# A gated linear recurrence and a squared-ReLU network on one core: a chunk's columns in another order, and the orders of VectorE and TensorE written by hand

## The chip, the core and the metric

The kernel runs on one core of a Trainium2 chip. Times are device microseconds (us) of one execution; the time of a kernel is the median of its runs. The engines are TensorE (PE; its weight loads are listed as PEld), VectorE (DVE), ScalarE (ACT), GpSimd (POOL) and SyncE (SP), which here issues transfers. Each works through its own list of instructions in order.

## What is computed

The reference, cut to what matters (batch 4, 8 heads, 768 steps, head size 48; the network takes 384 to 2048 to 384 over 3072 tokens):

```python
scale = np.minimum(mag, 0.999) / (mag + 1e-06)          # mag = |a_re + i a_im|
a_re_n, a_im_n = a_re * scale, a_im * scale
for t in range(S):
    new_re = ar * S_re - ai * S_im                      # ar, ai: step t of a_re_n, a_im_n
    new_im = ar * S_im + ai * S_re
    S_re, S_im = new_re + einsum('bhd,bhe->bhde', k[:, :, t], v[:, :, t]), new_im
    y[:, :, t] = einsum('bhd,bhde->bhe', q[:, :, t], S_re)
x = y with the heads side by side                       # 3072 x 384
h = np.maximum(x @ w_in, 0.0)
out = (h * h) @ w_out
```

## The kernel before

**Tiling.** A sequence of 768 steps is cut into 6 chunks of 128 steps (`C`). The 8 heads of a chunk lie as 4 pairs, a pair on 128 partitions with 48 rows and a gap of 16 for each head; the gaps of three pairs hold the rows of the fourth, so `NG` = 3 column blocks carry 4 pairs. Two chunks of different sequences make a group (`GC` = 2), so there are 12 groups (`NGR`), 256 tokens each; groups 0 to 5 run through one pair of sequences, 6 to 11 through the other. Within a chunk, 8 neighbouring steps make a block (`L` = 8, `NB` = 16 blocks).

**Operands of a group** (`make_operands`). ACT and DVE turn the gates of a group into running products along time. `steps_in_blocks` multiplies along a block, 7 steps in all, each a product `pr` of 384 elements and two writes of 96; the columns it takes, step `j` of every block, lie 8 elements apart in `raw`. A scan of 12 pieces makes the scale factors, four levels of doubling (`while m < NB`) join the 16 blocks of a chunk, ACT copies the carries, and a complex product over 1344 elements (`inner`) applies them. The last products write `qk`, the decayed queries and keys (four rows of 128 columns per block); six DMAs on SP's queue move the rows of the fourth pair into `last`.

**Attention of a chunk** (`chunk`, a generator with two stops). PE multiplies the state of the chunk before (`y<-qk,state_mm` and `y<-last,state_mm`), then queries and keys into the scores `a_ps`; DVE masks them into `a`; PE adds `a` times the values `vt` to `y`, and ACT copies `y` to `x`. Then PE transposes the keys (`tp`), ACT copies them to `kt`, PE makes `add`, and DVE joins it to the `state` (the last chunk of a sequence leaves this out).

**The network.** `first_product` makes `h_ps`, 8 pieces of 6 matrix products of 256 columns (each two passes in the trace), from `x`, whose gaps six DMAs fill (`fill_gaps`, `x<-x`); ACT applies ReLU and square. `second_product` makes `o_ps`, 16 products of 384 columns for each of the two chunks; ACT copies the result to `o`, and SP stores it. The weights come as 64-bit numbers; DVE decodes them in 16 pieces (`weights`, five instructions each), the first 8 for `h_ps`, the others for `o_ps`.

**What sets the order.** Through groups 0 and 1 DVE's list is the order of the code (`manual_schedule`); everything else, and DVE from group 2 on, is ordered by a scheduler. `attention(gi)`, `first_product(gi - 1)` and `second_product(gi - 1)` are written one after the other for each group.

**PSUM banks.** `a_ps` 2, `y` 1, `tp` and `add` together 2, `h_ps` 2, `o_ps` 1.

Of the kernel before, what the change touches and what calls it, by code (L numbers as in the profile page):

```python
# [11 lines left out]

# [402 lines left out]
def quotient_path(ctx, tc, feat, vtok, w_in, w_out, w1, w2, out, n_seq, good):  # L415
# [23 lines left out]
    tmp = ctx.enter_context(tc.tile_pool(name="tmp", bufs=1))  # L439
    att = ctx.enter_context(tc.tile_pool(name="att", bufs=2))  # L440
# [10 lines left out]
    def pads(hh):  # L451
        return gap_rows(hh, D)
# [10 lines left out]
    vt = [const.tile([C, HH * NP, ROWS], F32, name=f"vt{i}") for i in range(2 * GC)]  # L463
    for t in vt:
        nc.gpsimd.memset(t, 0.0)

    def load_parts(gi, parts, gaps):

        for b, n in enumerate(groups[gi]):
            for hh in range(HH):  # L470
                nc.sync.dma_start(
                    out=raw[gi % 2][rows(hh), parts, b].rearrange("d x g t -> d x (g t)"),
                    in_=feat[n, hh, :, parts, 0:NG].rearrange("d x g t -> d x (g t)"))
                rest = feat[n, hh].rearrange("(g r) x p t -> g r x p t", g=NG)
                for g in range(NG):
                    gaps.dma_start(out=raw[gi % 2][pads(hh), parts, b, g],
                                   in_=rest[g, :, parts, NG])

    def load_values(gi):
        for b, n in enumerate(groups[gi]):  # L480
            nc.sync.dma_start(out=vt[gi % 2 * GC + b][:, :, 0:D],
                              in_=vtok[n * C:(n + 1) * C].rearrange("c (h d) -> c h d", d=D))

    def load(gi):
        load_parts(gi, slice(A_RE, V), nc.sync)
        load_values(gi)

    load_parts(0, slice(A_RE, Q), nc.scalar)
    load_parts(0, slice(Q, V), nc.sync)
# [10 lines left out]
    nc.gpsimd.memset(mask, 1.0)  # L500
    nc.gpsimd.affine_select(out=mask, in_=mask, pattern=[[1, C]], compare_op=ALU.is_ge, fill=0.0,
                            base=0, channel_multiplier=-1)
# [98 lines left out]
    def make_operands(gi):  # L601
        r = raw[gi % 2].rearrange("p x b g t -> p x (b g t)")
        a = r[:, A_RE:A_IM + 1]
        ab = a.rearrange("p c (n j) -> p c n j", j=L)
        n = SEG * NB

        def steps_in_blocks(js):

            for j in js:
                x, w = ab[:, :, :, j - 1], ab[:, :, :, j]  # L610
# [13 lines left out]
                                       op1=ALU.add)  # L624
        nc.scalar.activation(out=z, in_=u, func=AF.Abs_reciprocal_sqrt)
# [13 lines left out]
                                       op1=ALU.mult)  # L639
        steps_in_blocks((5,))  # L640
        for x, y in ((u, low), (v, high)):
            for s in range(SEG):
                at = slice(s * C, (s + 1) * C)
                nc.vector.tensor_tensor_scan(out=x[:, at], data0=x[:, at], data1=y[:, at],  # L644
                                             initial=1.0, op0=ALU.mult, op1=ALU.mult)
        for i, x in enumerate((u, v)):
# [16 lines left out]
        inner = ab[:, :, :, 0:L - 1]  # L663
        cmul(inner, inner, spread(carry.rearrange("p c s n -> p c (s n)"), [n, L - 1]), [n, L - 1],
             [nrm.tile([P, 2, E], F32, tag=tag, name=tag)[:, :, 0:n * (L - 1)].rearrange(
                 "p c (n j) -> p c n j", j=L - 1) for tag in ("sq", "both")])

        qk, pd = qk_of[gi % 2], prod[gi % 2]
        shrink = ends[:, 0, gi].rearrange("p (b g) -> p b g", g=NG)
        for c in (RE, IM):  # L670
            tt(qk[:, c, :, :, C], raw[gi % 2][:, A_RE + c, :, :, C - 1], shrink, ALU.mult)
        steps = qk.rearrange("p x b g t -> p x (b g) t")[:, :, :, 0:C]
        a3 = a.rearrange("p x (s t) -> p x s t", t=C)
# [16 lines left out]
    def chunk(gi, b):  # L690
# [23 lines left out]
        yield  # L714
        am = []
        for hh in range(HH):
            am.append(att.tile([C, NP, C], F32, name="a", bufs=3))
            tt(am[hh], ps[hh], mask.unsqueeze(1).to_broadcast([C, NP, C]), ALU.mult)
        for p_ in range(NP):
            for hh in range(HH):  # L720
                nc.tensor.matmul(y[hh * ROWS:(hh + 1) * ROWS, p_], lhsT=v[:, HH * p_ + hh],  # L721
# [8 lines left out]

        for c in (RE, IM):
# [4 lines left out]
            nc.scalar.copy(  # L736
                out=kt[c][:, NG].rearrange("t (hh x) -> t hh x", hh=HH)[:, :, 0:D].rearrange(
                    "t hh (g r) -> t hh g r", g=NG),
                in_=tp.rearrange("t g (hh x) -> t hh g x", hh=HH)[:, :, :, D:ROWS])
        add = pm.tile([P, 2, NP, D], F32, tag="m", name="add")  # L740
        for c in (RE, IM):
            for p_ in range(NP):
                for hh in range(HH):
                    rr = slice(hh * ROWS, (hh + 1) * ROWS)
                    nc.tensor.matmul(add[rr, c, p_], lhsT=kt[c][:, p_, rr],  # L745
                                     rhs=v[:, HH * p_ + hh, 0:D], start=True, stop=True)
# [10 lines left out]
        p_ = tmp.tile([P, 2, NP, D], F32, tag="tp", name="p_")  # L757
# [38 lines left out]
    def store(i, b, ps):  # L796
# [3 lines left out]
        nc.sync.dma_start(out=out[n * C:(n + 1) * C], in_=o)  # L800

    def attention(gi):
        make_operands(gi)
        for b in range(GC):
            for _ in chunk(gi, b):
                pass
        if gi + 2 < NGR:
            load(gi + 2)
        fill_gaps(gi)

    def attention_among(gi, others):

        make_operands(gi)
        first, second = [chunk(gi, b) for b in range(GC)]
        for step, n in ((first, 3), (first, 0), (second, 2), (second, 0), (first, 1), (second, 0)):
            next(step, None)
            for _ in range(n):
                next(others)
        load(gi + 2)
        fill_gaps(gi)  # L820
# [3 lines left out]
    banks = {}  # L824

    def first_weights():
        for j in every:
            weights(j)
            yield

    def second_weights():
        for b, pool, tag in ((0, po, "o"), (1, ph, "h")):
            banks[b] = pool.tile([P, DM], F32, tag=tag, name="o_ps")
        for j in every:
            weights(NBLK + j)
            for b in range(GC):
                second_product(0, b, banks[b], [j])
            yield

    with tc.manual_schedule(engines={mybir.EngineType.DVE}):  # L840
        others = first_weights()
        attention_among(0, others)
        first_product(0, every[:6])
        for j in every[6:]:
            next(others)
            first_product(0, [j])
        others = second_weights()
        attention_among(1, others)
        for j in every[6:]:
            next(others)  # L850
            first_product(1, every[4 * (j - 6):4 * (j - 6) + 4])
        for b in range(GC):
            store(0, b, banks[b])
    for gi in range(2, NGR + 1):
        if gi < NGR:
            attention(gi)
# [79 lines left out]
```

## Time and profile before

| | |
|---|---|
| median of 3 runs | 823.46 us (821.85 to 823.92) |
| profiled execution | 823.65 us, of which the span of its trace is 821.9 us |
| mean granted clock of PE | 0.968 |
| PE busy | 695.2 us (85% of the span) |
| DVE busy | 497.7 us (61%) |
| ACT busy | 287.0 us (35%) |
| chain that ended last | PE 59%, DVE 31%, DMA 3%, issue 3%, ACT 3% |

Busy shares are means over stages of different kinds: decoding and first operands at the start, a mixture in the middle, matrix products alone at the end. PE's passes overlap, so a busy PE is not PE at its peak; where the text needs the cost of a pass it takes the start of one run of passes to the start of the next. A line L459 is the helper `tt`, by which nearly all DVE products are issued, so the rows go by tiles.

### The profile page before, as it was taken

What the parts mean: (1) busy time and instruction counts of PE and PEld (TensorE: products, weight loads), DVE (VectorE), ACT (ScalarE), POOL (GpSimd) and SP (SyncE); (2) the same over time, 40 slices, a digit from 0 to 9 for tenths busy, and PEclk for the clock granted to TensorE, in tenths of its full rate; (3) what the DMA queues carried; (4) which work ended last, traced back from release to release, by engine and by line L of the source; (5) the groups of instructions that cost most, each with busy time, mean ns of one, the idle gap of its engine ahead of it and who ended that gap; (6) DMA issues with size and microseconds to landing.
All of it is one profiled execution on the core that took longest, in us unless ns stands there. A gap on an engine that the chain in (4) does not pass through costs nothing.

```text
span 821.9 us, 10849 instructions
## 1 busy us (share of the span) xinstructions
PE 695.2 (85%) x4154; PEld 531.9 (65%) x4154; DVE 497.7 (61%) x1020; ACT 287.0 (35%) x558; POOL 7.7 (1%) x22
## 2 busy tenths in 40 slices
PE   0074319979897998998999989989999999999997
PEld 0063208658666866866858758768778678677673
DVE  4979999799798899999949479179113021010000
ACT  3145336335231624532525334334314224013130
POOL 3000000000000000000000000000000000000000
PEclk9999959999698999999999999999999999999999
DMA  5959807504324513242602501501002000000000
GB/s 122 161 101 187 165 7 167 125 15 78 48 59 82 84 38 78 53 82 45 105 17 46 82 24 32 86 23 34 12 20 45 10 10 6 10 14 2 20 0 25
DMA packets 68670, 47.65 MB, mean 58 GB/s; under 512 B 31616, under 2 KB 63488, under 8 KB 68608
## 3 DMA queue, kind: packets, MB, share of 16 engines
q1 hardware_dynamic: 68032, 46.66, 30.5%
q8 instruction: 35, 0.57, 0.3%
q10 hardware_dynamic: 576, 0.20, 0.1%
q14 instruction: 27, 0.22, 0.1%
HBM read 36.18 MB, written 4.72 MB: 50 GB/s over the span
## 4 chain that ended last, share of the span: by engine, by line
PE 59%; DVE 31%; DMA 3%; issue 3%; ACT 3%; SPq 1%; ACTq 0%; DVEq 0%
PE h_ps L782 25%; PE o_ps L793 22%; DVE raw L459 6%; DVE pr L459 5%; DVE sq L644 4%; PE a_ps L712 4%; PE y L721 3%; PE add L745 2%; DMA raw<-in_feat_dram 2%; PE y L705 2%; DVE a L459 2%; DVE qk L459 2%; DVE sq L459 1%; DVE both L544 1%; DVE state L459 1%
## 5 line engine op out<-in xcount | busy, mean ns | idle before, releaser
L782 PE MATMUL h_ps<-x,w 128*128 128x256 f32 x1152 | 262.5, 386 | 40.6 <-DMA x<-x 21.7
L782 PEld LDWEIGHTS h_ps<-x,w 128*128 128x128 f32 x1152 | 219.6, 193 | 75.6 <-issue 24.1
L793 PE MATMUL o_ps<-w,h 128*128 128x384 f32 x768 | 255.7, 491 | 4.3 <-DVE w L459 3.2
L793 PEld LDWEIGHTS o_ps<-w,h 128*128 128x128 f32 x768 | 145.2, 191 | 101.5 <-DVE w L459 3.3
L459 DVE TENSOR_TENSOR a<-a_ps,mask 128x512 f32<-128x512 f32 x48 | 30.9, 682 | 132.5 <-PE a_ps L712 132.5
L459 DVE TENSOR_TENSOR pr<-raw 128x384 f32<-128x384 f32 x84 | 71.7, 854 | 60.0 <-DMA raw<-in_feat_dram 59.0
L785 ACT ACTIVATE h<-h_ps 128x512 f32<-128x512 f32 x96 | 57.1, 594 | 91.6 <-PE h_ps L782 91.2
L712 PE MATMUL a_ps<-qk 48*128 48x128 f32 x576 | 51.1, 301 | 43.5 <-DVE qk L459 43.5
L712 PEld LDWEIGHTS a_ps<-qk 48*128 48x128 f32 x576 | 43.5, 203 | 49.8 <-DVE qk L459 43.5
L721 PE MATMUL y<-a,vt 128*64 128x128 f32 x384 | 41.6, 318 | 26.8 <-DVE a L459 26.7
L786 ACT ACTIVATE h<-h 128x512 f32<-128x512 f32 x96 | 60.4, 630 | 2.6
L799 ACT COPY o<-o_ps 128x384 f32<-128x384 f32 x24 | 11.5, 479 | 142.5 <-PE o_ps L793 142.4
L721 PEld LDWEIGHTS y<-a,vt 128*64 128x64 f32 x384 | 29.3, 157 | 37.0 <-DVE a L459 28.8
L459 DVE TENSOR_TENSOR raw<-pr 128x96 f32<-128x96 f32 x168 | 44.4, 331 | 8.0 <-ACT sq L619 6.2
L644 DVE TENSOR_TENSOR_SCAN sq<-sq,both 128x128 f32<-128x128 f32 x144 | 46.9, 400 | 1.1 <-ACT both L635 0.9
L901 DVE CAST count<-number 1x1 int32<-1x1 f32 x1 | 0.1, 145 | 72.5 <-PE number L900 72.5
L459 DVE TENSOR_TENSOR qk<-raw 128x1536 f32<-128x1536 f32 x24 | 41.5, 1752 | 1.4 <-PE a_ps L712 1.2
L745 PE MATMUL add<-vt,kt 128*64 128x48 f32 x640 | 34.4, 247 | 5.2 <-ACT kt L736 5.0
L726 ACT COPY x<-y 128x512 f32<-128x512 f32 x24 | 14.1, 587 | 67.3 <-PE y L721 67.3
L745 PEld LDWEIGHTS add<-vt,kt 128*64 128x64 f32 x640 | 31.3, 160 | 9.5 <-ACT kt L736 8.2
L705 PEld LDWEIGHTS y<-qk,state_mm 128*128 128x128 f32 x240 | 31.7, 198 | 5.6 <-ACT x L726 0.4
L765 ACT COPY state_mm<-state 48x384 f32<-48x384 f32 x40 | 20.4, 509 | 41.8 <-DVE state L459 41.6
(275 smaller groups left out, 578.4 us busy)
## 6 DMA issues: line engine op xcount, KB each, us to landing
raw<-in_feat_dram SPq DMA_DIRECT2D x44, 288.0 KB, 5.0
words<-in_moe_w_out_dram SPq DMA_DIRECT2D x8, 768.0 KB, 4.8
last<-qk SPq DMA_DIRECT2D x72, 64.5 KB, 2.5
vt<-in_vtok_dram SPq DMA_DIRECT2D x24, 192.0 KB, 3.3
words<-in_moe_w_in_dram SPq DMA_DIRECT2D x16, 288.0 KB, 8.1
out_dram<-o SPq DMA_DIRECT2D x24, 192.0 KB, 1.9
raw<-in_feat_dram SPq DMA_DIRECT2D x132, 32.0 KB, 4.6
words<-in_moe_w_in_dram SPq DMA_DIRECT2D x16, 96.0 KB, 8.5
```

The costliest lines, as they stand in the source:

```text
L459: nc.vector.tensor_tensor(out=out, in0=in0, in1=in1, op=op)
L644: nc.vector.tensor_tensor_scan(out=x[:, at], data0=x[:, at], data1=y[:, at], initial=1.0, op0=ALU.mult, op1=ALU.mult)
L705: nc.tensor.matmul(y[:, p_], lhsT=s[:, c, p_].rearrange("p hh e -> p (hh e)"), rhs=operand(c, p_, slice(0, P)), start=(p_ == 0 and c == RE ...
L712: nc.tensor.matmul(ps[hh][:, p_], lhsT=operand(2 + c, p_, rows(hh)), rhs=operand(c, p_, rows(hh)), start=(c == RE), stop=(c == IM))
L721: nc.tensor.matmul(y[hh * ROWS:(hh + 1) * ROWS, p_], lhsT=v[:, HH * p_ + hh], rhs=am[hh][:, p_], start=(first and p_ == 0), stop=(p_ == NP ...
L726: nc.scalar.copy(out=x_of[gi][:, :, b * C:(b + 1) * C], in_=y)
L745: nc.tensor.matmul(add[rr, c, p_], lhsT=kt[c][:, p_, rr], rhs=v[:, HH * p_ + hh, 0:D], start=True, stop=True)
L765: nc.scalar.copy(out=state_mm[b][rows(hh), :, :, hh, 0:D], in_=new[rows(hh)])
L782: nc.tensor.matmul(ps[:, j], lhsT=w1[:, g, (2 * f + j) * P:(2 * f + j + 1) * P], rhs=x_of[i][:, g], start=(g == 0), stop=(g == NG - 1))
L785: nc.scalar.activation(out=h, in_=ps, func=AF.Relu)
L786: nc.scalar.activation(out=h, in_=h, func=AF.Square)
L793: nc.tensor.matmul(ps, lhsT=h_of[i, f][:, j, b * C:(b + 1) * C], rhs=w2[:, k], start=(k == 0), stop=(k == NFB - 1))
```

## The change

The steps of a chunk stand in another order wherever they are columns or rows: first step 0 of all 16 blocks, then step 1 of all 16, and so on. `make_operands` copies `a` into a tile `ab` in this order (one ACT copy of 1536 elements) and queries and keys into `qk` (two of 768); `steps_in_blocks`, the levels and `inner` then work on neighbouring elements of `ab`, and the last products are four of 768 elements. The values `vt` are loaded and the results stored in the turned order of rows; `vt` drops its gaps between heads. The mask is turned at the start. The transposes of the keys are put ahead of the first stop of `chunk`, and `make_operands` becomes a generator with five stops.

DVE and PE now take everything in the order of the code. `front` writes out groups 0 and 1, `slot(gi)` everything after: attention of group `gi`, the network of group `gi - 1` and the operands of group `gi + 1` in pieces. ACT, POOL and SP stay with the scheduler.

```diff
+    prd = ctx.enter_context(tc.tile_pool(name="prd", bufs=1))
-    vt = [const.tile([C, HH * NP, ROWS], F32, name=f"vt{i}") for i in range(2 * GC)]
+    vt = [const.tile([C, DM + PAD], F32, name=f"vt{i}") for i in range(2 * GC)]
+    def in_turn(rows_, n):
+        return rows_[n * C:(n + 1) * C].rearrange("(n j) m -> j n m", j=L)
     def load_values(gi):
         for b, n in enumerate(groups[gi]):
-            nc.sync.dma_start(out=vt[gi % 2 * GC + b][:, :, 0:D],
-                              in_=vtok[n * C:(n + 1) * C].rearrange("c (h d) -> c h d", d=D))
+            nc.sync.dma_start(out=vt[gi % 2 * GC + b][:, 0:DM], in_=in_turn(vtok, n))
-    load_parts(0, slice(A_RE, Q), nc.scalar)
-    load_parts(0, slice(Q, V), nc.sync)
+    load_parts(0, slice(A_RE, Q), (nc.sync, nc.scalar))
+    load_parts(0, slice(Q, V), (nc.sync, nc.sync))
...
     def make_operands(gi):
-        ab = a.rearrange("p c (n j) -> p c n j", j=L)
+        ab = prd.tile([P, 2, L, n], F32, name="ab")
+        nc.scalar.copy(out=ab.rearrange("p c j n -> p c n j"),
+                       in_=a.rearrange("p c (n j) -> p c n j", j=L))
         def steps_in_blocks(js):
             for j in js:
-                x, w = ab[:, :, :, j - 1], ab[:, :, :, j]
+                x, w = ab[:, :, j - 1], ab[:, :, j]
...
         tt(r[:, Q], r[:, Q], u, ALU.mult)
         tt(r[:, K], r[:, K], v, ALU.mult)
+        by = [qk[:, i, :, :, 0:C].rearrange("p b g (j n) -> p (b g) j n", j=L) for i in range(4)]
+        for i, x in ((3, Q), (2, K)):
+            nc.scalar.copy(out=by[i].rearrange("p s j n -> p s n j"),
+                           in_=r[:, x].rearrange("p (s n j) -> p s n j", n=NB, j=L))
...
-        for i, x in enumerate((Q, K)):
-            by = r[:, x].rearrange("p (s t) -> p s t", t=C).unsqueeze(1)
-            tt(steps[:, 2 * i:2 * i + 2], a3, by.to_broadcast([P, 2, SEG, C]), ALU.mult)
+        tt(by[0], pv[RE], by[3], ALU.mult)
+        tt(by[1], pv[IM], by[3], ALU.mult)
+        tt(by[3], pv[IM], by[2], ALU.mult)
+        tt(by[2], pv[RE], by[2], ALU.mult)
...
+    def slot(gi):
+        done = gi == NGR
+        coming = make_operands(gi + 1) if gi + 1 < NGR else iter(())
+        chunks = iter(()), iter(())
+        if not done:
+            chunks = [chunk(gi, b) for b in range(GC)]
         if gi + 2 < NGR:
-            load(gi + 2)
+            load_parts(gi + 2, slice(A_RE, V), (nc.sync, nc.sync))
+        first_product(gi - 1, every[:4])
+        advance(chunks[0], 1)
+        advance(coming, 1)
+        first_product(gi - 1, every[4:])
+        advance(chunks[0], 1)
+        advance(chunks[1], 1)
+        advance(coming, 1)
+        advance(chunks[0], 1)
+        advance(coming, 1)
         for b in range(GC):
             ps = po.tile([P, DM], F32, tag="o", name="o_ps")
             second_product(gi - 1, b, ps, every)
             store(gi - 1, b, ps)
+            if b == 0:
+                advance(chunks[1], 1)
+                if not done:
+                    fill_gaps(gi)
+                advance(coming, 1)
+                advance(chunks[1], 1)
+                advance(coming)
+        if gi + 2 < NGR:
+            load_values(gi + 2)
+    def front():
...
+        advance(make_operands(0))
+        first, second = [chunk(0, b) for b in range(GC)]
+        advance(first, 1)
+        for j in every[:3]:
+            weights(j)
+        advance(first, 1)
+        advance(second, 1)
+        for j in every[3:5]:
+            weights(j)
+        advance(second, 1)
+        advance(first, 1)
+        weights(5)
+        advance(second, 1)
+        load(2)
+        fill_gaps(0)
+        first_product(0, every[:6])
+        for j in every[6:]:
+            weights(j)
+            first_product(0, [j])
+        advance(make_operands(1))
+        first, second = [chunk(1, b) for b in range(GC)]
+        advance(first, 1)
+        second_weights(every[:6])
+        advance(first, 1)
+        advance(second, 1)
+        second_weights(every[6:])
...
-    with tc.manual_schedule(engines={mybir.EngineType.DVE}):
...
+    with tc.manual_schedule(engines={mybir.EngineType.DVE, mybir.EngineType.PE}):
+        front()
+        for gi in range(2, NGR + 1):
+            slot(gi)
```

How the lists change is shown at three places; a number behind a name is the buffer's (`qk_171`/`qk_172` and `qk_179`/`qk_180` are the two operand buffers before and after).

PE before, from the scores of one chunk of a group in the middle (group 4) to the network of the group before it:

```order
L712 MATMUL a_ps<-last_173 128x128 x4
L734 MATMUL tp<-ident,qk_171 128x128 x6
L782 MATMUL h_ps<-x,w_58 128x256
L745 MATMUL add<-vt_99,kt_187 64x48 x5
L721 MATMUL y<-a,vt_99 64x128
L745 MATMUL add<-vt_99,kt_187 64x48 x3
L745 MATMUL add<-vt_99,kt_188 64x48 x5
L721 MATMUL y<-a,vt_99 64x128 x7
L745 MATMUL add<-vt_99,kt_188 64x48 x3
L782 MATMUL h_ps<-x,w_58 128x256 x46
L793 MATMUL o_ps<-w_59,h 128x384 x16
```

PE after, the slot of group 4 from its first network piece:

```order
L811 MATMUL h_ps<-x,w_58 128x256 x24
L734 MATMUL y<-qk_179,state_mm_187 128x128 x6
L734 MATMUL y<-last_181,state_mm_187 128x128 x2
L741 MATMUL a_ps<-qk_179 128x128 x12
L741 MATMUL a_ps<-last_181 128x128 x4
L746 MATMUL tp<-ident,qk_179 128x128 x6
L811 MATMUL h_ps<-x,w_58 128x256 x24
L760 MATMUL y<-a,vt_101 64x128 x8
L774 MATMUL add<-vt_101,kt_195 64x48 x8
L774 MATMUL add<-vt_101,kt_196 64x48 x8
```

The products of `y` and `add`, which wait for DVE's mask and ACT's `kt`, stood two or three instructions behind the scores; now half of `h_ps` (24 products) stands between.

DVE before, around the mask of a chunk of group 5 (the operands in the same rows are those of groups 7 and 8):

```order
L459 TENSOR_TENSOR pr<-raw_96 128x384
L459 TENSOR_TENSOR qk_172<-raw_97 128x12x128
L459 TENSOR_TENSOR a<-a_ps,mask 128x512 x2
L459 TENSOR_TENSOR qk_172<-raw_97 128x12x128
L459 TENSOR_TENSOR z<-z,sq 128x768
L459 TENSOR_TENSOR raw_96<-pr 128x96
```

DVE after, in the slot of group 3, from the state of its first chunk:

```order
L461 TENSOR_TENSOR state<-add,state 128x384
L461 TENSOR_TENSOR p__1845<-state,prod_184 128x384
L461 TENSOR_TENSOR w__1846<-state,prod_184 128x384
L461 TENSOR_TENSOR state<-p__1845,w__1846 128x192 x2
L461 TENSOR_TENSOR pr<-ab 128x384
L461 TENSOR_TENSOR ab<-pr 128x96 x2
L664 SCALAR_TENSOR_TENSOR sq<-sq,both 128x128 x12
L461 TENSOR_TENSOR a<-a_ps,mask 128x512 x2
```

The pieces of the next group's operands, here one step and the scans, stand between the steps of the chunks at places fixed by `slot`.

ACT after, at the border of two slots (the scheduler's order; `o` is the second store of the slot before, `ab` the copy for the operands two groups ahead of the network):

```order
L828 COPY o<-o_ps 128x384
L814 ACTIVATE h<-h_ps 128x512
L815 ACTIVATE h<-h 128x512
L621 COPY ab<-raw_99 128x2x96x8
L814 ACTIVATE h<-h_ps 128x512
L815 ACTIVATE h<-h 128x512
L814 ACTIVATE h<-h_ps 128x512
L644 ACTIVATE z<-sq 128x768
```

The copy into `ab`, which no list had before, stands ahead of the second ReLU of `h_ps`.

## Rows read from the trace of the kernel before

**Rows 1.** Stretches: us, busy us per engine (instructions), PEclk, DMA share, GB/s.
```profile
0.00:121.00 121.00, 31.31 (x197) 26.07 (x197) 101.06 (x192) 42.15 (x80) 7.71 (x22) 0.94 0.70 125
121.00:217.60 96.60, 88.28 (x545) 69.57 (x545) 85.94 (x163) 46.85 (x95) 0.00 (x0) 0.91 0.46 92
217.60:580.00 362.40, 339.62 (x2141) 260.51 (x2141) 290.70 (x632) 137.15 (x270) 0.00 (x0) 0.97 0.31 56
```
**Rows 2.** PE's waits, whole span: for whom, us in total, times, longest.
```profile
PE h_ps L782 <- DMA x<-x: 21.7, 1, 21.7
PE h_ps L782 <- ACT h L785: 18.9, 3, 18.0
```
**Rows 3.** PE's waits from 217 us on.
```profile
PE y L721 <- DVE a L459: 18.0, 9, 5.7
```
**Rows 4.** Groups by shape: out<-in, count | busy us, mean ns | idle before.
```profile
L459 DVE TENSOR_TENSOR pr<-raw 128x384 f32<-128x384 f32 x84 | 71.7, 854 | 60.0 <-DMA raw<-in_feat_dram 59.0
L459 DVE TENSOR_TENSOR raw<-pr 128x96 f32<-128x96 f32 x168 | 44.4, 331 | 8.0 <-ACT sq L619 6.2
L459 DVE TENSOR_TENSOR qk<-raw 128x1536 f32<-128x1536 f32 x24 | 41.5, 1752 | 1.4 <-PE a_ps L712 1.2
L459 DVE TENSOR_TENSOR state<-add,state 128x384 f32<-128x384 f32 x16 | 8.9, 554 | 13.5 <-PE add L745 13.4
...
L619 ACT ACTIVATE sq<-raw 128x1536 f32<-128x1536 f32 x12 | 17.8, 1482 | 24.5 <-DMA raw<-in_feat_dram 19.5 <-DVE raw L459 4.8
L661 ACT COPY carry<-raw 128x180 f32<-128x180 f32 x12 | 6.2, 515 | 45.0 <-DVE raw L459 44.9
```
**Rows 5.** Timeline, operands of groups 0 and 1: start, us, instruction.
```profile
43.41 0.55 DVE L537 TENSOR_SCALAR both<-words 128x768 int32<-128x768 int32 x1
...
87.26 0.84 DVE L459 TENSOR_TENSOR pr<-raw 128x384 f32<-128x384 f32 x1
...
116.85 3.42 DVE L459 TENSOR_TENSOR qk<-raw 128x1536 f32<-128x1536 f32 x2
...
120.19 0.55 DVE L537 TENSOR_SCALAR both<-words 128x768 int32<-128x768 int32 x1
...
120.33 3.89 SPq L680 DMA_DIRECT2D last<-qk  x6
```
**Rows 6.** Timeline, first instruction of two decodes in a row.
```profile
79.05 0.55 DVE L537 TENSOR_SCALAR both<-words 128x768 int32<-128x768 int32 x1
...
83.21 0.56 DVE L537 TENSOR_SCALAR both<-words 128x768 int32<-128x768 int32 x1
```
**Rows 7.** Chain of waits, one group near the end: start, us, what.
```profile
623.77 20.05 PE h_ps L782 x92
643.82 10.32 PE o_ps L793 x32
654.81 10.49 PE o_ps L793 x32
...
679.66 20.49 PE h_ps L782 x94
```
**Rows 8.** Timeline of PE, a chunk in that group.
```profile
671.89 1.61 PE L705 MATMUL y<-qk,state_mm 128*128 128x128 f32 x12
...
673.87 1.49 PE L712 MATMUL a_ps<-qk 48*128 48x128 f32 x21
...
675.85 0.88 PE L734 MATMUL tp<-ident,qk 128*128 128x128 f32 x6
...
678.52 1.13 PE L745 MATMUL add<-vt,kt 128*64 128x48 f32 x29
```
**Rows 9.** DMA issues (count, KB each, us to landing), and the end (timeline).
```profile
last<-qk SPq DMA_DIRECT2D x72, 64.5 KB, 2.5
...
x<-x SPq DMA_DIRECT2D x72, 16.0 KB, 1.8
...
816.53 0.48 ACT L799 COPY o<-o_ps 128x384 f32<-128x384 f32 x1 [10.68 <-PE o_ps L793]
```

More of the change, by code (lines that the diff above doesn't have):

```diff
@@ L462, in quotient_path, with load_parts @@
     raw = [const.tile([P, 4, GC, NG, C], F32, name=f"raw{i}") for i in range(2)]
[L463 removed]
+    vt = [const.tile([C, DM + PAD], F32, name=f"vt{i}") for i in range(2 * GC)]
     for t in vt:
[L465 to L467 removed]
+        nc.gpsimd.memset(t[:, DM:], 0.0)
+    def load_parts(gi, parts, queues):
         for b, n in enumerate(groups[gi]):
[L470 to L471 removed]
+            for hh, queue in enumerate(queues):
+                queue.dma_start(
                     out=raw[gi % 2][rows(hh), parts, b].rearrange("d x g t -> d x (g t)"),
@@ L713, in chunk @@
                                      rhs=operand(c, p_, rows(hh)), start=(c == RE), stop=(c == IM))
[L714 to L721, printed above, removed]
-                                 rhs=am[hh][:, p_], start=(first and p_ == 0),
-                                 stop=(p_ == NP - 1), skip_group_check=True)
-        if b == 0:
-            x_of[gi] = ffn.tile([P, NP, TOK], F32, name="x")
-        nc.scalar.copy(out=x_of[gi][:, :, b * C:(b + 1) * C], in_=y)
-        if final:
-            return
-        for c in (RE, IM):
+        for c in () if final else (RE, IM):
             tp = pm.tile([C, NG, P], F32, tag="m", name="tp")
@@ L739, in chunk @@
                 in_=tp.rearrange("t g (hh x) -> t hh g x", hh=HH)[:, :, :, D:ROWS])
+        yield
+        am = []
+        for hh in range(HH):
+            am.append(att.tile([C, NP, C], F32, name="a", bufs=2))
+            tt(am[hh], ps[hh], mask.unsqueeze(1).to_broadcast([C, NP, C]), ALU.mult)
+        for p_ in range(NP):
+            for hh in range(HH):
+                at = (HH * p_ + hh) * D
+                nc.tensor.matmul(y[hh * ROWS:(hh + 1) * ROWS, p_], lhsT=v[:, at:at + ROWS],
+                                 rhs=am[hh][:, p_], start=(first and p_ == 0),
+                                 stop=(p_ == NP - 1), skip_group_check=True)
+        if b == 0:
+            x_of[gi] = ffn.tile([P, NP, TOK], F32, name="x")
+        nc.scalar.copy(out=x_of[gi][:, :, b * C:(b + 1) * C], in_=y)
+        if final:
+            return
         add = pm.tile([P, 2, NP, D], F32, tag="m", name="add")
@@ L799, in store @@
         nc.scalar.copy(out=o, in_=ps)
[L800 to L806, printed above, removed]
-        if gi + 2 < NGR:
-            load(gi + 2)
[L809 to L820, printed above, removed]
@@ L823, in quotient_path @@
-    every = range(NFB // 2)
[L824 to L838, printed above, removed]
-    with tc.manual_schedule(engines={mybir.EngineType.DVE}):
[L841 to L853, printed above, removed]
@@ L854, in quotient_path, with advance @@
-    for gi in range(2, NGR + 1):
-        if gi < NGR:
-            attention(gi)
-        if gi > 2:
-            first_product(gi - 1, every)
+        nc.sync.dma_start(out=in_turn(out, n), in_=o)
+    every = range(NFB // 2)
+    def advance(steps, n=None):
+        for _ in itertools.islice(steps, n):
+            pass
+    def slot(gi):
[4 more added lines that the diff above has]
+            chunks = [chunk(gi, b) for b in range(GC)]
+        if gi + 2 < NGR:
+            load_parts(gi + 2, slice(A_RE, V), (nc.sync, nc.sync))
[8 more added lines that the diff above has]
+        advance(coming, 1)
```

66 lines of the change are left out of this document (50 added, 16 removed).

## The prediction

> **What bounds the kernel now.** I read the busy time by stretches first [rows 1], then what TensorE (PE) waited for [rows 2, 3], then the chain of waits where it runs dense [rows 7]. In the first 121 us VectorE (DVE) is busy 101 us and PE 31 us: the lead-in is DVE's. From 217.6 to 580 us PE is busy 339.6 of 362.4 us, so 22.8 us are lost to idling, at a granted clock of 0.97; most of it is the product `y` waiting for the masked scores `a` that DVE writes late (18.0 us in 9 waits) [rows 3]. Only near the end is PE alone the bound: from one `h_ps` to the next, 623.77 to 679.66, a whole group takes 55.89 us [rows 7]. There DVE has run out of work. So there are three things to gain: a shorter DVE chain ahead, PE's waits in the middle, and 0.67 us per group where the second `o_ps` waits for the bank of the first (643.82 + 10.32 against 654.81) [rows 7].
>
> **What the PE list costs without waits.** An `h_ps` pass is 20.49/94 = 0.218 us, 96 passes 20.9 us; the two `o_ps` are 10.32 us each. A full group is then 55.89 - 0.67 = 55.2 us, of which 13.7 are two chunks of attention: state product 1.98 us, scores 1.98, transposes about 0.75, `add` about 1.15, `y` the rest, 1.0 [rows 8]. A sequence's last group has no transposes and no `add` (51.4 us), its first no state product (51.3 us).
>
> **The change part by part.**
>
> *Contiguous columns.* In `steps_in_blocks` a product of 384 strided elements takes 854 ns, a contiguous one of 384 takes 554 ns; a strided write of 96 takes 331 ns, and the slope between 554 ns (384) and 1752 ns (1536), 1.04 ns per element, puts a contiguous 96 at about 255 ns [rows 4]. One step is one product and two writes: 0.30 + 0.15 us of busy time, some 0.38 us in the chain since the two writes overlap. Seven steps: 2.7 us per group. The four doubling levels are 16 small operations, 0.5 us in all. The big products over 1344 and 672 elements had seven of eight neighbours and the mask and scans are as before: nothing. The last products become four of 768 instead of two of 1536: by the same slope 4 x 0.95 against 2 x 1.75, +0.2 us in the chain. Net 3.0 us of DVE per group.
>
> *The copy that pays for it.* ScalarE (ACT) now writes `ab` from `raw`, 1536 elements, strided on the write side. No row shows that; the contiguous square of 1536 is 1.48 us, the strided `carry` copy of 180 takes 515 ns, 2.9 ns per element, which would make 4.4 us [rows 4]. DVE's strided rows cost not quite twice the contiguous ones, so I take twice the square, 3.0 us, and keep 1.5 to 4.4. Two more ACT copies of 768 (half of that) lie beside DVE's last steps and levels and wait for nothing. Group 0 pays the 3.0 us in the open, ahead of DVE's first step, but no longer waits there for the square, and its `a_re, a_im` loads are now split evenly over two queues: operands of group 0 end at 42.6 instead of 43.4 us [rows 5]. In a slot the copy waits until the previous group's last product has read `ab` (one buffer), and the second `h` ReLU stands behind it on ACT; the PE bank it holds comes back about 0.2 us late.
> The Trainium skill (ScalarE: Activation LUTs, What ACT_TABLE_LOAD costs) gives 186 ns plus 0.833 ns per element for such an instruction, which is 1.47 us for the copy; it would put `carry` at 336 ns where the trace has 515, so here the measurement decides; by the rule the sum below would be 1.5 us less.
>
> *The order.* DVE does the eight decodes of the first weights (4.16 us each [rows 6]) ahead of group 1's operands. From 42.6: 8 x 4.16 = 33.3, four masks 2.5, two states 4.6, about 1 us of waiting: 83.9 us (before: 87.26). Group 1's operands took 87.26 to 120.19, less one step of another group, 32.2 us [rows 5]; now 29.2: 113.1. The `h` ReLU of group 0 still stands on ACT behind a square that waits for these operands (the 18.0 us wait [rows 2] stays, but ends near 113 instead of 121), so PE ends `h_ps` of group 0 near 132, the attention of chunk 2 near 137. Six decodes end at 138, one mask pair 139.4. Now PE leads: 24 `o_ps` products of 10.32/16 = 0.645 us end at 153, `y`, `add` and the other chunk's scores at 160, eight more products, `y` and `add` at 167. DVE follows with state 1 at 169.4 and the rest of group 2's operands (29.2 less the 8.4 done by then): 190.2. `last` needs six DMA issues, 3.9 us, and 2.5 us to land [rows 5, 9]: 196.5. Meanwhile PE has done half of `h_ps` of group 1 (its fill landing near 173) and waits. So at 196.5 us PE goes on with `y<-last` of group 2.
>
> *From there.* Rest of that slot: 55.2 - 10.45 (half of `h_ps`) - 1.5 (the `qk` part of the state product, 12 of its 16 passes) = 43.3. PE stood still twice shortly before, and in 121 to 217.6 us the granted clock was 0.91 for such stops [rows 1], 8.7 us at half of which is lost around three of them: 2.5 us for these two, an estimate. Then six full slots 331.2, two last groups 102.8, one first 51.3, the closing slot 20.9 + 20.6 + 0.5 = 42.0: 527.3. Sum 196.5 + 43.3 + 2.5 + 527.3 = 769.6.
>
> *What may stand in PE's way in a slot.* The list puts other PE work over every DVE step: the masks lie under 10.45 us of `h_ps` or under an `o_ps`. The long way is: the second `add` ends 10.45 + 4.7 + 10.45 + 2.15 + 4.7 + 10.32 + 2.15 = 44.9 us into the slot; state 2.2, levels 3.4, carry copy 0.5, big products 4.6, last products 3.7 on DVE; `last` 6.4: 65.7. PE asks for it at 55.2 + 10.45 + 1.5 = 67.1. Slack 1.4 us, so it is covered, narrowly. `x<-x` follows the second `y`: 43.9, copy 0.6, six issues 3.9 (as for `last`), landing 1.8 [rows 9]: 50.2 of 55.2. I put 0.5 us a slot for ReLUs and issue gaps, 5 us in ten slots: 774.6. Behind PE's last pass the trace has 821.9 - 816.5 = 5.4 us [rows 9]: a span of 780.0. The profiled execution took 823.65 us with a span of 821.9, 1.75 us around it; it stands 0.2 us above the median 823.46. That makes 781.8, so **782 us**.
>
> Two smaller edits are nothing by themselves: `vt` in rows of 1536 bytes instead of 192 is a load that nobody waits for in time, and the store in turned order moves the same rows. The transpose of the mask at the start runs while PE has no work.
>
> **Rivals.**
> *The long way does not fit.* Its slack is 1.4 us; a `last` landing late, DVE behind its list or an ACT instruction in front of `carry` makes it 2 to 4 us longer. It counts at some eight slot borders: 8 x (0.6 to 2.6) = 5 to 21 us: 787 to 803. For it: seven waits of ACT and SP in one chain; against: each has a row.
> *The words come late.* All decodes and operands wait for DMA in the lead-in; 5 to 10 us more at 196.5: 787 to 792.
> *Strides were not the price* (the change doesn't do what it says): three groups' operands in the lead-in stay 3 us longer each: 791; the slots still cover them.
> *Better:* the copy at 1.5 us, no cold start, no gaps: 782 - 1.5 - 2.5 - 5 = 773, or down to 768 with the lead-in 5 us shorter.
> *Slower than before:* PE's list is fixed, so one late fill stops all. If `x<-x` goes out behind the store of the second `o_ps` on SP's queue, it starts at 55.9, lands at 61.6, and PE waits 6.4 us in each of ten slots: 782 + 64 = 846. It decides from 4.2 us per slot on. Against it: in the order of SP the fill stands right behind the store of the first.
>
> **How the numbers follow.** Forecast (777 to 788) 0.58; the long way 0.17; words 0.09; strides 0.03; better 0.10; slower 0.03. 782 is the time of the likeliest. Range 770 to 803: it leaves out the slower case, the ends of the long way and the best of the better ones. A measurement of this kernel tells 0.3% (2.5 us) from no change. Faster 0.96, same 0.01, slower 0.03.
>
> **What would show it.** Right: the strided product at about 555 ns and the writes at 255; the `ab` copy near 3 us; `y<-last` of group 2 at 190 to 203 us; from then PE busy over 98%, slots of 55 to 56 us; waits of `y` for `a` gone. Wrong: a PE wait for `last` in each slot (the long way), DVE idle for words ahead of 113 us, or PE standing for `x<-x`.

## The result, and the profile after

The changed kernel takes 776.72 us (median of 4 runs, 775.96 to 777.64) against 823.69 us for the one before: a ratio of 0.943 (0.939 to 0.946), 47 us less. 782 was forecast, with 770 to 803 around it. The profiled execution took 776.44 us with a span of 774.7.

Stretches of the changed kernel, cut as in [rows 1] but at the points that the prediction named (us, then busy us and instructions of PE, PEld, DVE, ACT and POOL, PEclk, DMA share, GB/s):

```profile
0.00:113.00 113.00, 28.51 (x207) 23.68 (x208) 97.21 (x197) 55.73 (x94) 6.02 (x22) 0.83 0.69 138
113.00:196.50 83.50, 68.31 (x432) 53.58 (x432) 67.89 (x129) 43.46 (x77) 0.00 (x0) 0.91 0.46 100
196.50:560.00 363.50, 361.21 (x2332) 278.63 (x2331) 230.24 (x538) 171.35 (x294) 0.00 (x0) 0.99 0.27 53
560.00:775.00 215.00, 206.39 (x1189) 156.72 (x1187) 80.87 (x183) 76.52 (x133) 0.00 (x0) 0.99 0.10 21
```

In the middle PE is now busy 361.2 of 363.5 us, where 22.8 of 362.4 us were lost [rows 1]. Its waits from 196 us on show what is left, and that none is for DVE's masks any more (18.0 us in [rows 3]):

```profile
PE y L734 <- ACT x L765: 3.1, 2, 2.3
PE o_ps L822 <- ACT o L828: 0.5, 1, 0.5
```

Stops are the smaller part of the gain. Busy times of the whole span:

```profile
PE 664.4 (86%) x4155; PEld 512.6 (66%) x4155; DVE 476.2 (61%) x1044; ACT 347.1 (45%) x596; POOL 6.0 (1%) x22
```

PE's busy time fell by 30.8 us, from 695.2, for the same passes; its idle time fell by 16.4 (span less busy: 126.7 before, 110.3 now). Two reasons for the shorter busy time can be read: the granted clock of the middle is 0.99, where it was 0.97 [rows 1], and a group without a stop takes 54.79 us, where it took 55.89 [rows 7], at a granted clock of 1.00 in both. How the 30.8 us divide is not separated.

The chain of waits, cut to the pieces of `h_ps` that begin a slot, answers to [rows 7] (start, us, what):

```profile
237.36 10.36 PE h_ps L811 x48
...
292.15 10.36 PE h_ps L811 x48
...
346.95 10.36 PE h_ps L811 x48
...
402.63 10.36 PE h_ps L811 x48
...
453.66 10.36 PE h_ps L811 x48
...
672.83 10.36 PE h_ps L811 x48
...
725.44 20.72 PE h_ps L811 x96
```

A full slot is 54.79 us (237.36 to 292.15). The slot of group 5, a sequence's last, is no shorter but longer (346.95 to 402.63, 55.68 us); the other last one takes 52.61 (672.83 to 725.44).

Groups of the changed kernel by shape, to lay beside [rows 4] (count | busy us, mean ns | idle before):

```profile
L461 DVE TENSOR_TENSOR pr<-ab 128x384 f32<-128x384 f32 x84 | 46.7, 555 | 39.1 <-ACT ab L621 37.5
...
L461 DVE TENSOR_TENSOR ab<-pr 128x96 f32<-128x96 f32 x168 | 35.9, 255 | 2.9
...
L621 ACT COPY ab<-raw 128x1536 f32<-128x1536 f32 x12 | 34.6, 2880 | 8.3 <-DVE qk L461 4.2 <-DMA words<-in_moe_w_in_dram 3.5
L674 ACT COPY qk<-raw 128x768 f32<-128x768 f32 x24 | 34.2, 1523 | 17.3 <-DVE raw L461 16.7 <-DMA raw<-in_feat_dram 0.7
...
L687 ACT COPY carry<-ab 128x180 f32<-128x180 f32 x12 | 4.1, 341 | 28.2 <-DVE ab L461 28.2
```

The products fell from 854 to 555 ns, the writes from 331 to 255. ACT pays with 2.88 us for the copy into `ab` and 1.52 for each of the two into `qk`.

The lead-in, from the timeline: the first instruction behind group 0's operands, the first of group 1's, the first behind them; then four places where PE goes on (in brackets what it waited for), and the first `o_ps`:

```profile
41.75 0.56 DVE L551 TENSOR_SCALAR both<-words 128x768 int32<-128x768 int32 x1
...
80.19 0.55 DVE L461 TENSOR_TENSOR pr<-ab 128x384 f32<-128x384 f32 x1
...
109.70 0.55 DVE L551 TENSOR_SCALAR both<-words 128x768 int32<-128x768 int32 x1
```

```profile
89.15 6.88 PE L811 MATMUL h_ps<-x,w 128*128 128x256 f32 x24 [20.70 <-DMA x<-x]
109.01 7.21 PE L811 MATMUL h_ps<-x,w 128*128 128x256 f32 x24 [12.98 <-ACT h L814]
...
131.61 15.65 PE L822 MATMUL o_ps<-w,h 128*128 128x384 f32 x48
...
166.32 12.73 PE L811 MATMUL h_ps<-x,w 128*128 128x256 f32 x48 [4.99 <-DMA x<-x]
...
190.57 1.19 PE L734 MATMUL y<-last,state_mm 128*128 128x128 f32 x4 [6.63 <-DMA last<-qk]
```

The stops at 89 and 109 us answer to [rows 2]: they became a little shorter (20.7 and 13.0 against 21.7 and 18.0) but did not go.

### The profile page after: what moved, and what is told of

It is laid out like the page before. It is cut to its first block, busy times and chain, and to the rows that moved or that the text cites. A ratio compares the mean times of both kernels' runs of the same rounds, so it can differ in the third digit from the quotient of the medians.

```text
span 774.7 us, 10894 instructions
## 1 busy us (share of the span) xinstructions
PE 664.4 (86%) x4155; PEld 512.6 (66%) x4155; DVE 476.2 (61%) x1044; ACT 347.1 (45%) x596; POOL 6.0 (1%) x22
## 4 chain that ended last, share of the span: by engine, by line
PE 74%; DVE 19%; DMA 2%; SPq 2%; ACT 1%; issue 1%; DVEq 0%; ACTq 0%
PE o_ps L822 30%; PE h_ps L811 27%; PE a_ps L741 6%; PE y L734 5%; PE y L760 3%; DVE ab L461 2%; PE add L774 2%; DVE sq L664 2%; DVE both L558 2%; DVE both L553 2%; PE tp L746 2%; DVE w L461 2%; DVE qk L461 1%; DMA raw<-in_feat_dram 1%; DVE pr L461 1%; DVE both L555 1%
## 5 line engine op out<-in xcount | busy, mean ns | idle before, releaser
L461 DVE TENSOR_TENSOR pr<-ab 128x384 f32<-128x384 f32 x84 | 46.7, 555 | 39.1 <-ACT ab L621 37.5
L741 PE MATMUL a_ps<-qk 48*128 48x128 f32 x576 | 41.5, 294 | 29.0 <-DVE qk L461 29.0
L461 DVE TENSOR_TENSOR state<-add,state 128x384 f32<-128x384 f32 x16 | 8.9, 558 | 80.3 <-PE add L774 80.3
L461 DVE TENSOR_TENSOR qk<-ab,qk 128x768 f32<-128x768 f32 x48 | 44.9, 955 | 0.8
L674 ACT COPY qk<-raw 128x768 f32<-128x768 f32 x24 | 34.2, 1523 | 17.3 <-DVE raw L461 16.7
L794 ACT COPY state_mm<-state 48x384 f32<-48x384 f32 x40 | 20.4, 510 | 47.0 <-DVE state L461 46.8
L621 ACT COPY ab<-raw 128x1536 f32<-128x1536 f32 x12 | 34.6, 2880 | 8.3 <-DVE qk L461 4.2
L734 PE MATMUL y<-qk,state_mm 128*128 128x128 f32 x240 | 32.3, 285 | 6.3 <-ACT x L765 3.3
L461 DVE TENSOR_TENSOR ab<-pr 128x96 f32<-128x96 f32 x168 | 35.9, 255 | 2.9
L637 ACT ACTIVATE sq<-raw 128x1536 f32<-128x1536 f32 x12 | 17.8, 1482 | 39.7 <-DVE ab L461 25.3
L760 PE MATMUL y<-a,vt 128*64 128x128 f32 x384 | 29.0, 291 | 6.1 <-DVE a L461 6.1
```

The source lines that it names most:

```text
L461: nc.vector.tensor_tensor(out=out, in0=in0, in1=in1, op=op)
L621: nc.scalar.copy(out=ab.rearrange("p c j n -> p c n j"), in_=a.rearrange("p c (n j) -> p c n j", j=L))
L674: nc.scalar.copy(out=by[i].rearrange("p s j n -> p s n j"), in_=r[:, x].rearrange("p (s n j) -> p s n j", n=NB, j=L))
L734: nc.tensor.matmul(y[:, p_], lhsT=s[:, c, p_].rearrange("p hh e -> p (hh e)"), rhs=operand(c, p_, slice(0, P)), start=(p_ == 0 and c == RE ...
L794: nc.scalar.copy(out=state_mm[b][rows(hh), :, :, hh, 0:D], in_=new[rows(hh)])
```

## Experiments

My theory after these traces: the written order makes most of the gain; the contiguous columns shorten only the lead-in; and the 5 us by which the forecast was too long lie ahead of 190 us. Rivals: the short steps are what fits the slots; or the layout gains by itself.

### One part without the other

*The order alone*: lists as after; columns, mask, values and stores in the order of before (the packed `vt` and the split first loads stay). The edit, cut:

```diff
-        ab = prd.tile([P, 2, L, n], F32, name="ab")
-        nc.scalar.copy(out=ab.rearrange("p c j n -> p c n j"),
-                       in_=a.rearrange("p c (n j) -> p c n j", j=L))
+        ab = a.rearrange("p c (n j) -> p c n j", j=L)
...
-        return rows_[n * C:(n + 1) * C].rearrange("(n j) m -> j n m", j=L)
+        return rows_[n * C:(n + 1) * C]
```

> The lists of VectorE and TensorE by hand as in the changed kernel, but the columns in the old order: steps on elements 8 apart, no copy into a tile of its own, mask, values and stores as before. Theory (the order makes the gain, contiguity only shortens the lead-in): the strided product is back at 854 ns and the writes at 331; group 0's operands end near 43.4 us, group 1's near 114, and the state product of group 2 takes its last pass near 198 us instead of 190.6. From there full slots of 54.8 us, since the steps lie under TensorE's work: 784 us (780 to 788). Rival A (the slots need the short steps: the slack of the long way, 1.4 us, is used up): slots of 55.5 to 57 us, 790 to 800. Rival B (strides cost nothing in the end): 777.

Measured: 783.26 us, ratio to before 0.952 (0.950 to 0.954). The timeline of PE in this run:

```profile
197.32 1.19 PE L716 MATMUL y<-last,state_mm 128*128 128x128 f32 x4 [4.77 <-DMA last<-qk]
...
244.00 10.52 PE L793 MATMUL h_ps<-x,w 128*128 128x256 f32 x48
...
298.79 10.52 PE L793 MATMUL h_ps<-x,w 128*128 128x256 f32 x48
```

The slot is 54.79 us here too, to the hundredth, though a product takes 852 ns again. The lead-in ends 6.75 us later than at 190.57. So 41 of the 47 us are the order's, and most of PE's shorter busy time comes with it (667.2 us here). The columns are worth 6.5 us. In the traces, 6.1 us apart, they gain 6.75 us ahead of the slots and 0.8 in the slot of group 5 (56.48 us here), and the turned store at the end takes 1.5 back (see below).

*The layout alone*: `make_operands`, mask, values and stores as after, everything in the order of before.

> The order of before (scheduler from group 2 on, its own lists for groups 0 and 1), but the columns turned as in the changed kernel, with the copies that belong to it. Theory: only the operands of groups 0 and 1 stand in the open there, some 3 us each less 0.5: 815 to 820 us, and TensorE's waits for the masked scores stay near 18 us from 217 us on. Rival (short steps also take the waits in the middle away): those waits below 8 us, and 800 to 808 us.

Measured: 825.08 us, ratio 1.0005 (0.998 to 1.003): nothing. Here my theory missed. The operands of group 1 do end 5.6 us earlier (114.6 us against 120.19 in [rows 5]), but this is given back later. PE's waits in this run:

```profile
PE o_ps L814 <- ACT o L820: 18.1, 8, 3.5
PE y L742 <- DVE a L460: 11.0, 4, 4.1
```

The waits for `a` did shrink, from 26.7 us over the whole span to 11.0 (from 217 us on, from 18.0 to 4.1): the rival's sign came true, its time did not. In their place PE waits 18.1 us in 8 places for the bank of `o_ps` (1.2 us before). The timeline of ACT, then of PE, at one of them:

```profile
523.67 2.79 ACT L667 COPY qk<-raw 128x768 f32<-128x768 f32 x2 [0.65 <-DVE raw L460]
526.26 0.51 ACT L820 COPY o<-o_ps 128x384 f32<-128x384 f32 x1
```

```profile
526.83 12.28 PE L814 MATMUL o_ps<-w,h 128*128 128x384 f32 x32 [3.52 <-ACT o L820]
```

The copy of `o` that frees the bank stands on ACT's list behind the two new copies, which themselves wait for DVE. To test this, that copy goes to DVE:

```diff
-        nc.scalar.copy(out=o, in_=ps)
+        nc.vector.tensor_copy(out=o, in_=ps)
```

> The run with the layout alone (825.1 us), but the copy of o_ps to o is on VectorE instead of ScalarE, about half a microsecond each, so that it no longer stands behind the copies of the new layout on ScalarE. Theory (these copies took back what the shorter steps gave: TensorE waited 18.1 us in 8 places for the o of ScalarE): those waits under 5 us, and 810 to 814 us. Rival (the middle is bound by something else, and the wait only moves): 821 to 826.

Measured: 808.38 us, ratio 0.980 (0.975 to 0.984). The time went the theory's way and past its range (810 to 814); the wait fell, but not below 5 us:

```profile
PE o_ps L814 <- DVE o L820: 10.3, 7, 3.7
```

The time fell by 16.7 us, more than this wait (7.8) and that for `a` (3.0, to 8.0); the rest isn't separated (PE's busy time fell too, from 697.8 to 692.5). So in the old order the copies on ACT, standing ahead of `o`, took back at least part of what the shorter steps gave. That this is the whole is not shown: the scheduler makes other lists once `o` is on DVE, and the kernel before was not run with that edit (PE waited only 1.2 us for that bank there).

### Is the hand-written list needed

```diff
-    with tc.manual_schedule(engines={mybir.EngineType.DVE, mybir.EngineType.PE}):
-        front()
-        for gi in range(2, NGR + 1):
-            slot(gi)
+    with tc.manual_schedule(engines={mybir.EngineType.DVE, mybir.EngineType.PE}):
+        front()
+    for gi in range(2, NGR + 1):
+        slot(gi)
```

> The changed kernel, in which only the lead-in (groups 0 and 1) keeps its lists by hand; from group 2 on the scheduler orders VectorE and TensorE from the same code. TensorE's list from the third slot on is then nearly the one by hand; VectorE's is not. Theory (what counts is that operands of the next group, attention and network are written in one slot): waits for the masked scores stay under 5 us, 778 to 788 us. Rival (the list by hand itself is needed): waits for scores or operands come back with 15 us or more, over 792 us.

Measured: 807.67 us, ratio 0.981 (0.979 to 0.984): the rival's time, but not its wait. The masks are not late (1.8 us in one wait from 196 us on). PE's largest wait from 196 us on, and the starts of two slots from its timeline, with one of a later slot:

```profile
PE h_ps L811 <- ACT h L814: 21.5, 9, 3.4
```

```profile
295.53 5.34 PE L811 MATMUL h_ps<-x,w 128*128 128x256 f32 x24
304.27 5.45 PE L811 MATMUL h_ps<-x,w 128*128 128x256 f32 x24 [3.40 <-ACT h L814]
...
353.99 5.34 PE L811 MATMUL h_ps<-x,w 128*128 128x256 f32 x24
...
652.04 8.30 PE L811 MATMUL h_ps<-x,w 128*128 128x256 f32 x24 [3.42 <-ACT h L814]
```

The slot that begins at 295.53 us takes 58.46 us (full slots 56.3 to 61.3), 3.4 of them for the ReLU, which stands on ACT behind copies that wait for DVE (the copies into `qk` run from 301.01, the ReLU at 303.61). ACT's list is the scheduler's in both kernels, and it changes with the others: with DVE and PE by hand, the ReLU does not come late. Why the scheduler orders ACT so was not tested, nor DVE's list without PE's. From the same code without the lists, 31 of the 47 us are lost: 21.5 are this wait, and behind two of the stops the passes are slower too (8.30 us at 652.04 against 5.45 at 304.27).

### How near the slots are to their bound

The long way of the prediction (second `add`, state, levels, `last`, the state product of the next slot) was delayed by idle products on DVE ahead of the big products; *k* is 2 or 7:

```diff
+        for _ in range(k if gi > 2 else 0):
+            idle = tmp.tile([P, 2, 2, n], F32, tag="pr", name="idle")
+            tt(idle, ab[:, :, 0].unsqueeze(1).to_broadcast([P, 2, 2, n]),
+               ab[:, :, 1].unsqueeze(2).to_broadcast([P, 2, 2, n]), ALU.mult)
         inner = [P, 2, L - 1, n]
```

> The changed kernel with two idle products of 384 elements (some 0.58 us each, 1.2 us) on VectorE ahead of the big products of every group from group 3 on, that is on the long way from the second add of a slot to the pass of the next slot that reads last. Theory (the slack there is 1.4 us): nothing shows, slots of 54.8 us, 776 to 778 us. Rival (there is no slack left): 1.2 us in each of 8 slot borders, 786 us.

> The same with seven idle products, 4.1 us. Theory (slack of 1.4 us): TensorE waits for last some 2.7 us at 8 slot borders, 21 us, 798 us; with the passes behind such a stop at the lower clock, as behind the 2.3 us stop of the changed kernel at 375 us, up to 811. Rival (the cover is over 4 us): no wait for last, 776 to 778.

Measured: 777.88 us with 1.15 us of delay, 804.56 with 4.11. The small delay costs no wait for `last`, but its slots are 55.21 us, 0.42 longer: `ab` is copied 1.4 us later, and the second ReLU of `h_ps` stands behind it on ACT (at 300.24 us; in the changed kernel at 298.84, for a slot that begins 0.8 us earlier). The large delay, PE's waits from 230 us on and two slot starts:

```profile
PE y L738 <- DMA last<-qk: 15.1, 8, 2.8
```

```profile
237.54 10.52 PE L815 MATMUL h_ps<-x,w 128*128 128x256 f32 x48
...
296.03 10.52 PE L815 MATMUL h_ps<-x,w 128*128 128x256 f32 x48
```

Eight waits of 1.9 us on average, for 4.11 us of delay: the slack is some 2.2 us, where the prediction had 1.4. The time rose by 27.8, more than the 15.1 of the waits; the passes behind a stop are slower here. The stretch behind one:

```profile
251.26:255.83 4.57, 4.57 (x42) 4.22 (x43) 1.24 (x3) 2.13 (x6) 0.00 (x0) 0.70 0.01 4
```

The same passes take 3.23 us in the changed kernel (303.69 to 306.92). A mean granted clock of 0.70 means that part of this stretch ran at the lower of its two levels, 1.2 instead of 2.4 GHz.

### What was still to be had

*The fill of group 0.* PE stands until 89.15 us for `x<-x`, which SP issues only at 84.8, behind the loads of group 2.

```diff
-        load(2)
         fill_gaps(0)
+        load(2)
```

> The changed kernel with two lines of the lead-in exchanged: the fill of the gaps of x for group 0 stands ahead of the loads of group 2 on SP's queue. Theory (TensorE's waits in the lead-in, 20.7 us for the fill and 13.0 for ScalarE's ReLU, are what makes VectorE idle by some 6 us between 144 and 162 us): the first network product near 73 us instead of 89, both waits gone or under 5 us, the last pass of the state product of group 2 at 184 to 187 us instead of 190.6, and 771 us (769 to 774). Rival (VectorE alone sets the lead-in): VectorE's idle time stays and the time is 776 to 777.

Measured: 772.05 us, ratio 0.938 (0.936 to 0.940). PE's timeline:

```profile
79.04 10.39 PE L811 MATMUL h_ps<-x,w 128*128 128x256 f32 x36 [11.38 <-DMA x<-x]
...
186.96 1.20 PE L734 MATMUL y<-last,state_mm 128*128 128x128 f32 x4 [6.20 <-DMA last<-qk]
```

The fill comes 10 us earlier (16 had been expected; SP is busy with the loads of words until 70), PE's waits for the ReLU shrink from 13.3 to 2.3 us, since the ReLUs now come ahead of the square on ACT, and 4.7 us are gained. How PE's early waits reach the end shows in DVE's waits for PE between 110 and 190 us, first in the changed kernel, then here:

```profile
DVE state L461 <- PE add L774: 3.0, 2, 2.3
```

```profile
DVE state L461 <- PE add L774: 0.6, 1, 0.6
```

In the changed kernel there was also one of 1.9 us for the scores; here there is none.

*The slots of the last groups.* The changed kernel at 371 to 381 us: PE's timeline, then its stretch:

```profile
374.95 2.52 PE L734 MATMUL y<-qk,state_mm 128*128 128x128 f32 x12 [2.29 <-ACT x L765]
```

```profile
374.95:380.50 5.55, 5.55 (x48) 5.21 (x48) 0.00 (x0) 0.00 (x0) 0.00 (x0) 0.69 0.04 16
```

Without `add` nothing stands on PE between the `y` of the first chunk and the state product of the second, which needs the same bank.

```diff
-        first_product(gi - 1, every[4:])
+        ends_here = not done and groups[gi][0] % NCH == NCH - 1
+        at = 7 if ends_here else 8
+        first_product(gi - 1, every[4:at])
         advance(chunks[0], 1)
+        first_product(gi - 1, every[at:])
         advance(chunks[1], 1)
```

> The changed kernel, but in the slots of a sequence's last group one piece of the network (6 products of 256 columns, two passes each, 2.6 us) is moved from ahead of the first chunk's y to behind it, so that TensorE has work while ScalarE copies that y out of its one bank. Theory (the wait for this copy, and the passes at the lower clock behind it, are what makes the slot of group 5 55.7 us instead of 51.4, and that of group 11 52.6): both waits gone, both slots 51.2 to 51.8 us, 771 to 772.5 us. Rival (the copy stands behind ReLUs whatever TensorE does): the waits stay, 775 to 777.

Measured: 771.78 us, ratio 0.936 (0.934 to 0.939). Both waits are gone and both slots are 51.7 us:

```profile
346.62 10.52 PE L811 MATMUL h_ps<-x,w 128*128 128x256 f32 x48
...
398.35 10.52 PE L811 MATMUL h_ps<-x,w 128*128 128x256 f32 x48
```

*Both together.* 

> The changed kernel with both edits that gained alone: the fill of group 0 ahead of the loads of group 2 (772.1 us alone), and in the slots of a sequence's last group one piece of the network behind the first chunk's y (771.8 alone). Theory (the one lies in the lead-in, the other in two slots, and they share nothing): the gains add, 776.7 - 4.7 - 4.9 = 767.1 us (766.3 to 768). Rival (the one takes part of the other): 769 to 771.

Measured: 767.30 us, ratio 0.930 (0.926 to 0.934); the gains add up, and this beats both kernels.

*The copy's stride on the other side.*

```diff
-        nc.scalar.copy(out=ab.rearrange("p c j n -> p c n j"),
-                       in_=a.rearrange("p c (n j) -> p c n j", j=L))
+        nc.scalar.copy(out=ab, in_=a.rearrange("p c (n j) -> p c j n", j=L))
```

(and the copies into `qk` likewise)

> The changed kernel, but ScalarE's copies into the new order (ab, 1536 elements, and two of 768) write neighbouring elements and read 8 apart, instead of the other way round. Theory (a stride costs the same on either side): 2.88 and 1.52 us as before, 776 to 778 us. Rival (only strided writes are slow): 1.48 and 0.85 us, the operands of group 0 end 1.4 us earlier, 774 to 776.

Measured: 777.17 us, ratio 0.942 (0.940 to 0.944), no difference. A strided read costs about as much as a strided write (2.99 us against 2.88):

```profile
L621 ACT COPY ab<-raw 128x1536 f32<-128x1536 f32 x12 | 35.8, 2985 | 8.3 <-DVE qk L461 7.7
```

*The table load ahead of the gates*, on top of both edits that gained:

```diff
+    early = const.tile([P, 1], F32, name="early")
+    nc.scalar.copy(out=early, in_=ones)
```

> The same, with one copy of a single column on ScalarE at the start, from a tile that is there at 1 us, so that the table load of 1.28 us, which stands at 8.9 us behind the wait for the gates, is done while they are under way. Theory (from there to the state product of group 2 VectorE waits for nobody longer than 1 us): everything 1.3 us earlier, 765.8 us (765.3 to 766.4). Rival (the early part waits for something else, the gates of the second half or the mask): 767.

Measured: 767.01 us (765.79 to 767.24) against 767.30 (766.50 to 767.89): not to be told apart. DVE begins 1.1 us earlier, at 11.31 us, but `last` of group 2 is issued at 180.03 us instead of 179.94. DVE's wait for `add` in the lead-in (0.3 us without the edit):

```profile
DVE state L461 <- PE add L777: 1.5, 1, 1.5
```

The expectation's "VectorE waits for nobody" was wrong: with the other edits made, PE is as late as DVE there.

## Why the prediction was near, and where it was off

The prediction's sum, term by term, against the trace (us; the 0.5 us a slot is in the slots):

| term | forecast | measured |
|---|---|---|
| operands of group 0 end | 42.6 | 41.75 |
| operands of group 1 begin, end | 83.9, 113.1 | 80.19, 109.70 |
| last product of group 2 ends | 190.2 | 184.5 |
| PE goes on with `y<-last` | 196.5 | 190.57 |
| rest of that slot, with the slower passes | 46.3 | 46.8 |
| six full slots | 334.2 | 328.8 |
| two last groups' | 103.8 | 108.3 |
| one first group's | 51.8 | 51.0 |
| closing slot | 42.0 | 42.2 |
| behind the last pass | 5.4 | 7.1 |
| span | 780.0 | 774.7 |

**Right.** The mechanism: a lead-in that DVE sets, then slots that are PE's list and nothing else. DVE's prices (555 and 255 ns were forecast as 554 and 255), the copy into `ab` (3.0 forecast, 2.88), the length of group 1's operands (29.2; 29.5), the ReLU that stays stuck behind the square. Right in kind, but too small: the passes behind the last stop ran at a mean granted clock of 0.50 from 190.57 to 196.75 us, and the rest of that slot took 3.5 us more than the same part of a full slot (46.8 against 43.3), where 2.5 had been put down. The Trainium skill (ScalarE: Activation LUTs, What ACT_TABLE_LOAD costs) would put the copy at 1.47 us, an estimate by its rule; the trace has twice that. For `carry`, which now reads neighbours, its 336 ns agree with 341: by these rows the rule holds for neighbouring elements only.

**Off: the lead-in, 5.9 us too long.** This is the step that made 782 of 776.7. Of it, 0.85 us is group 0's operands. Another 2.9 lie between 41.75 and 80.19: the two states were priced at 2.3 us each from the row with the `add` to a state before, but a sequence's first chunk has none, and they take 1.6; the 1 us of waiting was not there; the eight decodes ran 0.4 us shorter. From 109.7 to the state at 163.7 PE leads, as forecast, in 54.0 us instead of 56.3. 2.0 of these 2.3 us lie ahead of the first `o_ps` (21.9 us behind 109.7, at 131.61; forecast 23.9, at 137): the network of group 0 goes on 0.7 us before the operands end, not behind them, and takes 18.0 us, where 19 had been put down. Against that, group 1's operands took 0.3 us longer. The rest is `last` from its last product on (6.07; 6.3).

**Off: the slots.** 0.5 us was added for ReLUs and issue gaps; the slot of 54.79 us has none, it is even shorter than the 55.2 taken from [rows 7]. That 55.2 rests on a wrong reading: the 0.67 us taken off as a wait between the two `o_ps` are six passes of the next chunk's state product, as the chain of the kernel before has it:

```profile
654.14 0.67 PE y L705 x6
```

So the old list took 55.89 us without a wait, and the new one 1.1 us less for the same passes; it keeps them in longer runs, but that this is the reason was not tested. Against that, the slots of last groups were forecast from PE's list (51.4) without asking who frees the bank of `y`; the run with one piece moved shows that this cost 4.8 us. The two errors nearly cancel (1.7 us), which is luck.

**Off: the store.** It does move the same rows, but that was no reason to price it at nothing. Behind the last ACT copy the changed kernel takes 7.0 us, the run with the order alone 5.5. The share of DMA in that tail, in 40 slices, first of the changed kernel (767.6 to 774.7 us), then of the order alone (775.2 to 780.8):

```profile
DMA  0000000010454524554030000000000010000000
```

```profile
DMA  0000000000999730000000000000200010000000
```

The turned store keeps about half of the 16 engines busy at most, the other nearly all. The Trainium skill (DMA: Bandwidth & Descriptors, Rules for kernel authors) says that a transfer whose outermost dimension is smaller than 16 goes to at most so many engines; the turned rows have 8 outermost, and the trace agrees. Only the last store is in the open; none of PE's waits is for one.

**Overlooked.** PE's 21.7 us for `x<-x` stand in [rows 2], and the prediction priced only the row below it. Bringing the fill 10 us forward was worth 4.7 us. The account of the gain names only stops and DVE's steps; the busy time of PE, 30.8 of the 47 us, comes into the forecast by the dense slots alone.

**The rivals.** The long way fits, with some 2.2 us of slack. The words were in time: DVE does not idle for them between 41.75 and 109.70. Without the contiguous columns the time is 783.3, not 791: the three groups lose 6.75 us, not 9, since the copy of group 0 is saved, and the last store is faster. The fill in the slots was in time: PE has no wait for `x<-x` from 196 us on. Of the better case (768 to 773) two parts came true, a lead-in more than 5 us shorter and full slots without gaps; the last groups' slots took most of the second back.

## What to carry to other kernels

Price a layout change with the copy that makes it, and look where that copy stands on its engine and what stands behind it; here the same layout was worth nothing in one order and 6.5 us in the other. Once one engine is to run without a stop, go through its list and ask at each place who frees the bank and when; a stop can cost more than its length. When a time is summed up in a lead-in, the waits of the engine that is *not* the bound are worth a look too: they set when the bound engine gets its next input.

## What the runs showed of the hardware that was not expected

- Elements 8 apart (32 bytes) cost ACT about twice, on either side: 2.88 us written and 2.99 read so, against 1.48 for the contiguous square of 1536.
- A stop of PE of 2.29 us was followed by 5.55 us at a mean granted clock of 0.69; the same passes without the stop took 3.87 us (372.52 to 376.39 in the run with one piece moved). One of 1.86 us was followed by 4.57 us at 0.70, against 3.23. It is not so behind every stop: in the run without the lists, 24 passes behind a stop of 3.40 us took 5.45 us at a granted clock of 1.00, and the same behind one of 3.42 us took 8.30 at 0.64. What decides between them is not shown.
- A store of 128 rows of 1536 bytes in turned order took the end of the kernel about 1.5 us longer than in the order of memory: 7.0 us from the last ACT copy to the end against 5.5.
